# Pinning TensorE's order around seven block products, and taking up the first bank's sum behind the third copy

## The chip, the cores and the metric

The kernel runs on one core of a Trainium2 chip. The time is the device time of the whole program in microseconds (us); lower is better. TensorE (PE) multiplies matrices into PSUM banks, VectorE (DVE) and ScalarE (ACT) do elementwise work, and SyncE (SP) issues the transfers. Each engine takes its instructions in a fixed order and waits at an instruction until its operands are ready.

## The reference

Two batches of 768 tokens pass a decayed block attention ("retention", 8 heads of 64), and its output goes through two feed-forward layers, one with Mish and one with ELU:

```python
x = attn_out.transpose(0, 2, 1, 3).reshape(1536, 512)
h = x @ moe_w_in                     # 512 -> 2048
g = h * np.tanh(softplus(h))         # Mish
x = g @ moe_w_out                    # 2048 -> 512
h = x @ moe2_w_in
g = np.where(h > 0, h, np.exp(np.minimum(h, 0)) - 1)   # ELU
return g @ moe2_w_out
```

## The kernel before

**Products.** Tokens come in three blocks of 512 (t = 0, 1, 2). Every operand is kept as two fp32r tiles, high part and low part, and each 128x128 by 128x512 product is made of three matmuls: high by high, high by low, low by high. In the text "a product" means one such matmul of 512 columns; a bank is one 128x512 PSUM tile.

**Groups and units.** A layer's 2048 inner columns are four groups of four slices of 128. A group's work is cut into units in the list `seq`: an `in` unit multiplies one slice of w_in with one token block (12 products, bank `h`, line 487), an `out` unit adds four slices through w_out (12 products, bank `y`, line 615), followed by an add into `acc` on VectorE (line 643).

**Seven block products.** In groups 1 to 3 of the first layer, token blocks 1 and 2 are not taken by `in` units. A pair of slices z (0 or 1) of a group is done by seven block products of 6 matmuls each (`block_product`, line 574), from sums of weights (tiles `s`) and sums of tokens (tiles `t2` to `t4`). They stand in four `mix` units, `MIX = ((1, 2), (6, 5), (7,), (4, 3))`. Bank 0 takes products 1, 6, 7 and 4 one on top of the other; behind 1, 6 and 7 ScalarE copies it away (`keep`, line 583), so 6 waits for the copy of 1, 7 for the copy of 6, and 4 for the copy of 7. Bank 1 takes product 2, bank 2 takes 5 and 3. `done` (line 587) adds a bank to a copy on VectorE, applies Mish on ScalarE and splits the result in two (`split_g`, line 161 for the low part). For z = 0 the banks come from the `y` pool and are called `mby`, for z = 1 from the `h` pool, `mbh`.

In `seq` the units of such a group stand as: `in` 0, 1, 2; mix 0 to 2 of z = 0; `in` 3; mix 3; `out` 0, 1, 2 of token block 0; mix 0 to 2 of z = 1; `out` 3; mix 3; then the other `out` units.

**Weights.** A pair of weight slices is loaded raw (512 KB a slice) and split in two by `w_steps`: VectorE lines 119, 123, 125, 129, 132, 136 and 139, then ScalarE line 143 writes the high part, then VectorE line 146 the low part. `w0` is a pair of w_in slices, `w1` a pair of w_out slices. The tables `PAIRS` and `at` say after which unit a pair is begun.

**Order.** A scheduler lays out each engine's instructions ahead of time: an instruction that it takes to be not ready yet lets later ones go first. An instruction marked with `keep_in_program_order` keeps its place against the other marked ones of its engine. Before the change only the attention's instructions are marked.

Of the kernel before, what the change touches and what calls it, by code (L numbers as in the profile page):

```python
# [18 lines left out]
def kernel(  # L19
# [12 lines left out]
    nc = tc.nc  # L32
# [430 lines left out]
    def open_late():  # L463
# [11 lines left out]
            )  # L475
        acc.extend(late["y"].tile([P, KD, TB], F32, name=f"acc{t}") for t in range(NTB))

    def mm_in(s, i):
        l, g, t = steps[s]
        w = wts[l, 0, g * G + i]  # L480
        h = (late["psH"] if entered[0] % 4 else psH).tile([P, TB], F32, tag="h", name="h")
        entered[0] += 1
        for kk in range(KD):
            wa, wb = (w[:, n, kk * P:(kk + 1) * P] for n in range(2))
            xa, xb = xh[t][:, kk], xl[t][:, kk]
            for n, (lt, rt) in enumerate(((wa, xa), (wa, xb), (wb, xa))):
                nc.tensor.matmul(  # L487
                    h, lhsT=lt, rhs=rt,
                    start=(kk == 0 and n == 0), stop=(kk == KD - 1 and n == 2),
                )  # L490
        return h
# [11 lines left out]
    def split_g(s, i):  # L503
        g, gg = mid.pop((s, i)), g_tile(s, i)
        in_two((gg[:, 0], gg[:, 1]), g)
        gt[s, i] = gg

    def mish(s, i, h):
        mid[s, i] = tp.tile([P, TB], F32, tag="e", name="g32", bufs=ES)
        nc.scalar.activation(out=mid[s, i], in_=h, func=AF.Mish)  # L510
# [10 lines left out]
    mx = {}  # L521
# [30 lines left out]
    def block_product(g, z, x):  # L552


        w = [wts[0, 0, g * G + 2 * z + j] for j in range(2)]
        sm = sums[g, z]
        def of(j, h):
            return [w[j][:, n, h * 2 * P:(h + 1) * 2 * P] for n in range(2)]
        a = {1: of(0, 0), 2: of(0, 1), 4: of(1, 1)}.get(x)
        if a is None:  # L560
            y = {5: 0, 6: 1, 7: 2, 3: 3}[x]
            a = [sm[:, n, y] for n in range(2)]
        b = mx["b"][x]
        bank = {1: 0, 6: 0, 7: 0, 4: 0, 2: 1, 5: 2, 3: 2}[x]
        fresh = x in (1, 2, 5)
        if fresh:
            pool, tag = ((late["psY"], "y"), (late["psH"], "h"))[z]
            mx[z, bank] = pool.tile([P, TB], F32, tag=tag, name="mb" + tag)
        ps = mx[z, bank]
        for kk in range(2):  # L570
            ha, la = (t[:, kk * P:(kk + 1) * P] for t in a)
            hb, lb = (t[:, kk] for t in b)
            for n, (lt, rt) in enumerate(((ha, hb), (ha, lb), (la, hb))):
                nc.tensor.matmul(  # L574
                    ps, lhsT=lt, rhs=rt, start=fresh and kk == 0 and n == 0,
                    stop=kk == 1 and n == 2, skip_group_check=True,
                )
        s1, s2 = g * NTB + 1, g * NTB + 2
        i1, i2 = 2 * z, 2 * z + 1

        def keep(y):
            mx[z, "c", y] = tp.tile([P, TB], F32, tag="e", name="c", bufs=ES)
            nc.scalar.activation(out=mx[z, "c", y], in_=ps, func=AF.Copy)  # L583

        def done(y, s, i):
            c = mx[z, "c", y]
            nc.vector.tensor_tensor(out=c, in0=c, in1=ps, op=ALU.add)
            nc.scalar.activation(out=c, in_=c, func=AF.Mish)
            mid[s, i] = c
            split_g(s, i)  # L590

        if x in (1, 6, 7):
            keep({1: 1, 6: 2, 7: 3}[x])
        if x == 2:
            done(1, s1, i1)
        elif x == 3:
            done(2, s2, i1)
        elif x == 4:
            mish(s1, i2, ps)
            split_g(s1, i2)  # L600
        if x == 7:
            ps = mx[z, 2]
            done(3, s2, i2)

    def mm_out(s, d, cols):
        l, g, t = steps[s]
        y = late["psY"].tile([P, TB], F32, tag="y", name="y")[:, cols]
        for i in range(G):
            w = wts[l, 1, g * G + i]
            gg = gt[s, i]  # L610
            a, b = (w, gg) if l == 0 else (gg, w)
            a = [a[:, n, d * P:(d + 1) * P] for n in range(2)]
            b = [b[:, n, cols] for n in range(2)]
            for n, (lt, rt) in enumerate(((a[0], b[0]), (a[0], b[1]), (a[1], b[0]))):
                nc.tensor.matmul(  # L615
                    y, lhsT=lt, rhs=rt,
                    start=(i == 0 and n == 0), stop=(i == G - 1 and n == 2),
                )
        return y

    def all_out(s):

        l, g, t = steps[s]
        ys = [late["psY"].tile([P, TB], F32, tag="y", name="y") for _ in range(KD)]
        for i in range(G):
            w, gg = wts[l, 1, g * G + i], gt[s, i]
            for d, y in enumerate(ys):
                a = [w[:, n, d * P:(d + 1) * P] for n in range(2)]
                for n, (lt, rt) in enumerate(((a[0], gg[:, 0]), (a[0], gg[:, 1]), (a[1], gg[:, 0]))):
                    nc.tensor.matmul(  # L630
                        y, lhsT=lt, rhs=rt,
                        start=(i == 0 and n == 0), stop=(i == G - 1 and n == 2),
                    )
        for d, y in enumerate(ys):
            flush(s, d, slice(0, TB), y)

    def flush(s, d, cols, y):
        l, g, t = steps[s]
        dst = acc[t][:, d, cols]
        if g == 0:  # L640
            nc.scalar.activation(out=dst, in_=y, func=AF.Copy)  # L641
        else:
            nc.vector.tensor_tensor(out=dst, in0=dst, in1=y, op=ALU.add)  # L643
        if g < NG - 1:
            return
        if l == 0:
            nc.scalar.activation(out=xh[t][:, d], in_=dst, func=AF.Copy)
            nc.vector.tensor_tensor(
                out=xl[t][:, d], in0=dst, in1=xh[t][:, d].bitcast(F32), op=ALU.subtract
            )  # L650
        else:
            c2, b = divmod(d, B)
            r0 = b * S + (2 * t + c2) * P
            nc.sync.dma_start(out=out[r0:r0 + P, cols], in_=dst)
# [3 lines left out]
    seq = [("in", t, i) for i in range(G) for t in range(NTB)]  # L658
# [8 lines left out]
    for g in range(1, NG):  # L667
        s = g * NTB
# [15 lines left out]

    def unit(u):
        kind, s, x = seq[u]
        if kind == "mix":
            for y in MIX[x]:
                block_product(*s, y)
        elif kind == "in":  # L690
            (mish, elu)[steps[s][0]](s, x, mm_in(s, x))
            if late:
                split_g(s, x)
        else:

            if s == 0:
                if x == 0:
                    all_out(s)
                return
            ends = (0, 3 * TB // 4, TB) if u == len(seq) - 1 else (0, TB)  # L700
            for c0, c1 in zip(ends, ends[1:]):
                cols = slice(c0, c1)
                flush(s, x, cols, mm_out(s, x, cols))
# [11 lines left out]
    for g in range(2 * NG):  # L715
        for y in range(4):
            u = PAIRS[g][y] if g in PAIRS else 92 + (g - 4) * 24 + (-18, -6, -9, -3)[y]
# [38 lines left out]
    def first_units():  # L756
        with tc.issue_after(made[-2].ins):
            for _ in todo:
                pass
        for u in range(EARLY):  # L760
            unit(u)
            weights_at(u)
# [5 lines left out]
    for u in range(EARLY, len(seq)):  # L768
        unit(u)
        weights_at(u)  # L770
# [32 lines left out]
```

## Time and profile before

| | |
|---|---|
| median of 3 runs | 576.34 us (576.29 to 577.77) |
| profiled execution | 576.26 us |
| its span, first to last instruction | 573.7 us |
| TensorE busy | 567.1 us, 99% |
| VectorE busy | 455.3 us, 79% |
| ScalarE busy | 246.0 us, 43% |
| granted TensorE clock | 1.000 |

Shares are of the span. 2.56 us of the execution lie outside the span. A busy share is a mean over stages; the attention takes the first 54 us, the first layer runs to some 340 us, the second to the end.

### The profile page before, as it was taken

The page shows a single profiled execution, that of the slowest core. Times are in us where ns is not written, and L with a number is a line of the kernel's source. Part 1 is how long each engine was busy: PE and PEld are TensorE (multiplying, and loading weights), DVE is VectorE, ACT ScalarE, POOL GpSimd, SP SyncE. Part 2 cuts the span into 40 slices and gives each one's busy share as a digit, 9 for nine tenths or more (in the row PEclk, how much of TensorE's full clock was granted, in tenths as well). Part 3 has the DMA queues.
Part 4 walks back from the last instruction along what each step waited for, and adds up shares of the span by engine and source line. Part 5 has one row for each costly group of instructions (what it writes and reads, how often), then busy time and mean ns, then how long its engine had stood idle before and what let it go on. Part 6 is the DMA issues. An engine that isn't in the chain of part 4 may idle for free.

```text
span 573.7 us, 7842 instructions
## 1 busy us (share of the span) xinstructions
PE 567.1 (99%) x3198; PEld 474.7 (83%) x3198; DVE 455.3 (79%) x628; ACT 246.0 (43%) x389; POOL 18.8 (3%) x28
## 2 busy tenths in 40 slices
PE   8999999999999999999999999999999999999997
PEld 7998888887888888888888888888888888888886
DVE  7779999999999979889989899898999634244232
ACT  3655553453542352422646447445325425225220
POOL 5330000000000000000000000000000000000000
PEclk9999999999999999999999999999999999999999
DMA  9998242111312421032222204404312000000112
GB/s 188 200 209 217 81 140 74 73 75 61 93 67 75 146 75 37 37 121 83 90 75 72 75 0 148 146 1 147 100 48 74 0 1 0 1 0 1 73 56 91
DMA packets 61042, 46.63 MB, mean 81 GB/s; under 512 B 38864, under 2 KB 55504, under 8 KB 61008
## 3 DMA queue, kind: packets, MB, share of 16 engines
q1 hardware_dynamic: 60864, 46.14, 26.7%
q8 instruction: 25, 0.41, 0.3%
q14 instruction: 9, 0.07, 0.0%
q10 hardware_dynamic: 144, 0.00, 0.0%
HBM read 43.00 MB, written 3.15 MB: 80 GB/s over the span
## 4 chain that ended last, share of the span: by engine, by line
PE 97%; SPq 1%; DMA 1%; issue 0%; ACT 0%; DVE 0%
PE y L615 44%; PE h L487 34%; PE mby L574 5%; PE mbh L574 5%; PE o L341 4%; PE y L630 2%; PE sc L327 2%; SPq L205 1%; DMA qn<-in_q_dram 1%; PE Tp L283 1%; PE st L373 1%; ACT c L583 0%; DVE acc L643 0%
## 5 line engine op out<-in xcount | busy, mean ns | idle before, releaser
L487 PE MATMUL h<-xh,w 128*128 128x512 f32 x576 | 181.7, 389 | 0.0
L615 PE MATMUL y<-w,g 128*128 128x512 f32 (+2 forms) x588 | 133.5, 386 | 0.0
L615 PEld LDWEIGHTS y<-w,g 128*128 128x128 f32 x588 | 109.5, 188 | 22.0
L487 PEld LDWEIGHTS h<-xh,w 128*128 128x128 f32 x576 | 108.1, 188 | 22.6 <-issue 0.2
L615 PE MATMUL y<-g,w 128*128 128x512 f32 x528 | 124.9, 389 | 0.0
L615 PEld LDWEIGHTS y<-g,w 128*128 128x128 f32 x528 | 99.1, 188 | 20.6
L487 PE MATMUL h<-xl,w 128*128 128x512 f32 x288 | 112.0, 389 | 0.0
L643 DVE TENSOR_TENSOR acc<-acc,y 128x512 f32<-128x512 f32 (+1 forms) x73 | 48.8, 677 | 41.5 <-PE y L615 41.4
L514 ACT ACTIVATE e<-h 128x512 f32<-128x512 f32 x48 | 28.6, 598 | 87.5 <-PE h L487 85.8
L487 PEld LDWEIGHTS h<-xl,w 128*128 128x128 f32 x288 | 54.1, 188 | 11.2
L516 DVE SCALAR_TENSOR_TENSOR e<-e,h 128x512 f32<-128x512 f32 x48 | 32.7, 685 | 25.9 <-ACT e L515 25.9
L146 DVE TENSOR_TENSOR w<-m,w 128x1024 fp32r<-128x1024 f32 (+2 forms) x35 | 39.5, 1130 | 8.5 <-ACT w L143 8.5
L143 ACT ACTIVATE w<-m 128x1024 fp32r<-128x1024 f32 (+2 forms) x35 | 34.4, 983 | 24.6 <-PE y L615 16.6
L161 DVE TENSOR_TENSOR g<-e,g 128x512 fp32r<-128x512 f32 x48 | 33.0, 689 | 12.2 <-ACT g L160 12.0
L160 ACT ACTIVATE g<-e 128x512 fp32r<-128x512 f32 x48 | 30.2, 630 | 24.3 <-DVE e L516 24.1
L129 DVE SCALAR_TENSOR_TENSOR raw<-raw,m 128x1024 int32<-128x1024 int32 (+2 forms) x35 | 39.4, 1130 | 0.2
L136 DVE SCALAR_TENSOR_TENSOR m<-raw,m 128x1024 f32<-128x1024 uint32 (+2 forms) x35 | 39.2, 1129 | 0.2
L139 DVE TENSOR_TENSOR m<-raw,m 128x1024 f32<-128x1024 f32 (+2 forms) x35 | 39.1, 1128 | 0.2
L510 ACT ACTIVATE g<-h 128x512 f32<-128x512 f32 x24 | 14.4, 598 | 44.8 <-PE h L487 44.8
L515 ACT ACTIVATE e<-e 128x512 f32<-128x512 f32 x48 | 30.0, 630 | 1.1
L641 ACT ACTIVATE acc<-y 128x512 f32<-128x512 f32 x24 | 13.9, 599 | 28.2 <-PE y L615 21.7
L119 DVE TENSOR_SCALAR m<-raw 128x1024 int32<-128x1024 int32 (+2 forms) x35 | 22.1, 644 | 3.5 <-DMA raw<-in_moe_w_out_dram 2.1
(105 smaller groups left out, 576.6 us busy)
## 6 DMA issues: line engine op xcount, KB each, us to landing
raw<-in_moe_w_out_dram SPq DMA_DIRECT2D x32, 512.0 KB, 4.1
raw<-in_moe_w_in_dram SPq DMA_DIRECT2D x31, 512.0 KB, 4.9
vn<-in_v_dram SPq DMA_DIRECT2D x12, 256.0 KB, 5.6
kn<-in_k_dram SPq DMA_DIRECT2D x11, 256.0 KB, 5.1
qn<-in_q_dram SPq DMA_DIRECT2D x11, 256.0 KB, 5.4
out_dram<-acc SPq DMA_DIRECT2D x11, 256.0 KB, 2.0
raw<-in_moe_w_in_dram SPq DMA_DIRECT2D x2, 256.0 KB, 4.9
kn<-in_k_dram SPq DMA_DIRECT2D x2, 128.0 KB, 3.3
```

Source lines behind the costliest of these rows:

```text
L129: yield nc.vector.scalar_tensor_tensor(out=b, in0=b, scalar=-0x40000000, in1=m, op0=ALU.bitwise_and, op1=ALU.bitwise_or)
L136: yield nc.vector.scalar_tensor_tensor(out=mf, in0=lw, scalar=2.0 ** -52, in1=mf, op0=ALU.mult, op1=ALU.mult)
L139: yield nc.vector.tensor_tensor(out=mf, in0=bf, in1=mf, op=ALU.add)
L143: nc.scalar.activation(out=w0, in_=mf, func=AF.Copy)
L146: yield nc.vector.tensor_tensor(out=w1, in0=mf, in1=w0.bitcast(F32), op=ALU.subtract)
L160: nc.scalar.activation(out=t[0], in_=x, func=AF.Copy)
L161: nc.vector.tensor_tensor(out=t[1], in0=x, in1=t[0].bitcast(F32), op=ALU.subtract)
L487: nc.tensor.matmul(h, lhsT=lt, rhs=rt, start=(kk == 0 and n == 0), stop=(kk == KD - 1 and n == 2),)
L516: nc.vector.scalar_tensor_tensor(out=e, in0=e, scalar=-1.0, in1=h, op0=ALU.add, op1=ALU.max)
L574: nc.tensor.matmul(ps, lhsT=lt, rhs=rt, start=fresh and kk == 0 and n == 0, stop=kk == 1 and n == 2, skip_group_check=True,)
L615: nc.tensor.matmul(y, lhsT=lt, rhs=rt, start=(i == 0 and n == 0), stop=(i == G - 1 and n == 2),)
L643: nc.vector.tensor_tensor(out=dst, in0=dst, in1=y, op=ALU.add)
```

## The change

A list `fixed` is filled while a unit is written out if that unit, the one ahead of it in `seq` or the one behind it is a `mix` unit. In that case each product of the unit is marked to keep program order. And `done(1)`, which adds bank 1 to the first copy, is called behind the third copy (after product 7) and not right after product 2.

```diff
+    fixed = []
+
+    def product(*args, **kw):
+        ins = nc.tensor.matmul(*args, **kw)
+        if fixed:
+            tc.keep_in_program_order(ins)
+
     def mm_in(s, i):
...
-                nc.tensor.matmul(
+                product(
...
         if x in (1, 6, 7):
             keep({1: 1, 6: 2, 7: 3}[x])
-        if x == 2:
-            done(1, s1, i1)
-        elif x == 3:
+        if x == 3:
             done(2, s2, i1)
         elif x == 4:
             mish(s1, i2, ps)
             split_g(s1, i2)
         if x == 7:
-            ps = mx[z, 2]
-            done(3, s2, i2)
+            for y, bank, s, i in ((3, 2, s2, i2), (1, 1, s1, i1)):
+                ps = mx[z, bank]
+                done(y, s, i)
...
     def unit(u):
         kind, s, x = seq[u]
+        fixed[:] = [1 for y in seq[max(u - 1, 0):u + 2] if y[0] == "mix"]
```

`mm_in`, `block_product` and `mm_out` call `product` in place of the matmul. The number of instructions on each engine stays the same, and so does the order up to the first mix unit of group 1. Lines shift: 487, 574 and 615 print as 481 in the order of the changed kernel, 583 as 590, 587 as 594, 643 as 649.

**Place one: TensorE, group 1, the first `out` units (`y_1701`, `y_1715`, `y_1729`).** `w1_1530` and `w1_1580` are the group's two pairs of w_out slices, `g_...` the split slices of token block 0; the third product of a slice is the first that reads the low part of its weights. Before:

```order
L574 MATMUL mby_1612<-t3_1298,s_1392 128x512 x6
L615 MATMUL y_1701<-g_1559,w1_1530 128x512 x2
L615 MATMUL y_1715<-g_1559,w1_1530 128x512 x2
L574 MATMUL mby_1612<-t4_1299,w0_1374 128x512 x6
L574 MATMUL mbh_1772<-xh2_66,s_1414 128x512
L574 MATMUL mbh_1772<-xl2_69,s_1414 128x512
L574 MATMUL mbh_1772<-xh2_66,s_1414 128x512 x2
L574 MATMUL mbh_1772<-xl2_69,s_1414 128x512
L574 MATMUL mbh_1772<-xh2_66,s_1414 128x512
L615 MATMUL y_1701<-g_1559,w1_1530 128x512
```

Now:

```order
L481 MATMUL y_1701<-g_1559,w1_1530 128x512 x2
L481 MATMUL y_1715<-g_1559,w1_1530 128x512 x2
L481 MATMUL y_1701<-g_1559,w1_1530 128x512
L481 MATMUL y_1701<-g_1577,w1_1530 128x512 x3
L481 MATMUL y_1701<-g_1609,w1_1580 128x512 x2
L481 MATMUL y_1715<-g_1559,w1_1530 128x512
L481 MATMUL y_1715<-g_1577,w1_1530 128x512 x3
L481 MATMUL y_1715<-g_1609,w1_1580 128x512 x2
```

The mix products that stood between the second and the third product of `y_1701` have moved ahead of it (z = 0) or behind it (z = 1), and the second pair of w_out slices is read 8 products after the first and not 39. Before, the first product after the group's `in` units 0 and 1 was product 1 of the mix; now the `in` unit 2 (`h_1594`, weights `w0_1396`) stands there whole. From that place to the first `y_1701` are 66 products in both kernels, and to its third product, the first that reads the low part of `w1_1530`, 70 products now.

**Place two: TensorE, group 1, the first `in` unit of group 2 (`h_1998`, weights `w0_1792`).** Before:

```order
L574 MATMUL mbh_1743<-t3_1298,s_1414 128x512 x6
L615 MATMUL y_1850<-g_1630,w1_1530 128x512 x3
L615 MATMUL y_1850<-g_1687,w1_1530 128x512 x3
L615 MATMUL y_1850<-g_1761,w1_1580 128x512 x3
L487 MATMUL h_1998<-xh0_64,w0_1792 128x512
L487 MATMUL h_1998<-xl0_67,w0_1792 128x512
```

Now:

```order
L481 MATMUL mbh_1752<-xh1_65,w0_1396 128x512 x2
L481 MATMUL mbh_1752<-xl1_68,w0_1396 128x512
L481 MATMUL mbh_1752<-xh1_65,w0_1396 128x512
L481 MATMUL h_1998<-xh0_64,w0_1792 128x512
L481 MATMUL h_1998<-xl0_67,w0_1792 128x512
L481 MATMUL mbh_1743<-t2_1297,s_1414 128x512 x6
```

It begins 39 products earlier, between products 2 and 6 of z = 1. From the third product of `y_1701` to it are 44 products (10 of `y_1701`, 10 of `y_1715`, 12 of `y_1729`, 12 of `mbh`).

**Place three: VectorE, up to the low part of `w1_1530`.** Before:

```order
L161 TENSOR_TENSOR g_1609<-g32_1607,g_1609 128x512
L132 TENSOR_SCALAR m_1581<-raw_1405 128x1024
L139 TENSOR_TENSOR m_1531<-raw_1383,m_1531 128x1024
L161 TENSOR_TENSOR g_1630<-c_1619,g_1630 128x512
L136 SCALAR_TENSOR_TENSOR m_1581<-raw_1405,m_1581 128x1024
L146 TENSOR_TENSOR w1_1530<-m_1531,w1_1530 128x1024
```

Now (`g_1609` stands further ahead, `g_1630` is called `g_1658`):

```order
L594 TENSOR_TENSOR c_1649<-c_1649,mby_1636 128x512
L132 TENSOR_SCALAR m_1581<-raw_1405 128x1024
L139 TENSOR_TENSOR m_1531<-raw_1383,m_1531 128x1024
L136 SCALAR_TENSOR_TENSOR m_1581<-raw_1405,m_1581 128x1024
L161 TENSOR_TENSOR g_1653<-c_1649,g_1653 128x512
L161 TENSOR_TENSOR g_1658<-c_1619,g_1658 128x512
L594 TENSOR_TENSOR c_1634<-c_1634,mby_1636 128x512
L161 TENSOR_TENSOR g_1676<-g32_1674,g_1676 128x512
L139 TENSOR_TENSOR m_1581<-raw_1405,m_1581 128x1024
L146 TENSOR_TENSOR w1_1530<-m_1531,w1_1530 128x1024
```

From the low part of `w0_1396` on, the instructions ahead of this line 146 are those of before and five more: the adds `c_1649` and `c_1634`, the splits `g_1653` and `g_1676`, and line 139 of `m_1581`. Behind it follow two splits (`g_1687`, `g_1698`), line 146 of `w1_1580`, and the steps of `w0_1792`: lines 119, 123, 125, 129, an add, 132, an add, 136, 139.

## Rows read from the trace of the kernel before

**Rows 1.** The page's span and busy times.

```profile
span 573.7 us, 7842 instructions
PE 567.1 (99%) x3198; PEld 474.7 (83%) x3198; DVE 455.3 (79%) x628; ACT 246.0 (43%) x389; POOL 18.8 (3%) x28
```

**Rows 2.** Chain that ended last: start us, length us, what.

```profile
137.86 1.37 PE mby L574 x6
139.90 1.65 PE mby L574 x6
142.47 1.43 PE mby L574 x6
...
179.05 10.88 PE y L615 x48
...
270.85 1.44 PE mby L574 x6
...
428.70 10.88 PE h L487 x48
```

**Rows 3.** Busy time by stretch: each engine's us and count, clock, DMA share, GB/s.

```profile
9.00:10.00 1.00, 0.52 (x7) 0.33 (x6) 1.00 (x2) 0.73 (x1) 1.00 (x2) 1.00 1.34 224
126.00:138.00 12.00, 12.00 (x55) 9.94 (x54) 11.79 (x17) 4.71 (x8) 0.00 (x0) 1.00 0.01 3
138.00:146.00 8.00, 7.31 (x32) 5.59 (x31) 7.21 (x10) 4.70 (x8) 0.00 (x0) 1.00 0.54 166
146.00:160.00 14.00, 14.00 (x63) 11.60 (x62) 13.96 (x21) 6.50 (x11) 0.00 (x0) 1.00 0.36 126
```

**Rows 4.** TensorE's timeline in group 1: start us, length us, what, idle before.

```profile
125.45 0.39 PE L574 MATMUL mby<-xh,w 128*128 128x512 f32 x1
...
137.69 1.52 PE L574 MATMUL mby<-t,s 128*128 128x512 f32 x6
139.90 1.65 PE L574 MATMUL mby<-t,s 128*128 128x512 f32 x6 [0.69 <-ACT c L583]
141.39 1.07 PE L615 MATMUL y<-g,w 128*128 128x512 f32 x4
```

**Rows 5.** ScalarE's timeline in the same place.

```profile
124.10 1.05 ACT L143 ACTIVATE w<-m 128x1024 fp32r<-128x1024 f32 x1
...
139.25 0.60 ACT L583 ACTIVATE c<-mby 128x512 f32<-128x512 f32 x1 [2.06 <-PE mby L574]
139.75 1.05 ACT L143 ACTIVATE w<-m 128x1024 fp32r<-128x1024 f32 x1
```

**Rows 6.** VectorE's timeline in group 1.

```profile
119.22 0.69 DVE L132 TENSOR_SCALAR m<-raw 128x1024 int32<-128x1024 int32 x1
119.94 1.23 DVE L136 SCALAR_TENSOR_TENSOR m<-raw,m 128x1024 f32<-128x1024 uint32 x1
121.20 1.22 DVE L139 TENSOR_TENSOR m<-raw,m 128x1024 f32<-128x1024 f32 x1
...
125.18 1.23 DVE L146 TENSOR_TENSOR w<-m,w 128x1024 fp32r<-128x1024 f32 x1
...
139.25 0.68 DVE L161 TENSOR_TENSOR g<-c,g 128x512 fp32r<-128x512 f32 x1
139.86 1.22 DVE L136 SCALAR_TENSOR_TENSOR m<-raw,m 128x1024 f32<-128x1024 uint32 x1
140.99 1.22 DVE L146 TENSOR_TENSOR w<-m,w 128x1024 fp32r<-128x1024 f32 x1
...
146.54 1.22 DVE L146 TENSOR_TENSOR w<-m,w 128x1024 fp32r<-128x1024 f32 x1
```

**Rows 7.** VectorE and TensorE at the mix of group 3.

```profile
259.14 0.68 DVE L587 TENSOR_TENSOR c<-c,mby 128x512 f32<-128x512 f32 x1
...
255.73 0.39 PE L574 MATMUL mby<-xh,w 128*128 128x512 f32 x1
```

**Rows 8.** TensorE's timeline at the start of the attention.

```profile
1.05 3.36 PE L267 MATMUL warm<-idle 128*128 128x128 f32 x14 [1.05 <-DVE idle L218]
4.34 0.47 PE L283 MATMUL Tp<-ident,kn 64*128 64x64 f32 x4
...
8.59 0.71 PE L267 MATMUL warm<-idle 128*128 128x128 f32 x4
```

More of the change, by code (lines that the diff above doesn't have):

```diff
@@ L573, in block_product @@
             for n, (lt, rt) in enumerate(((ha, hb), (ha, lb), (la, hb))):
-                nc.tensor.matmul(
+                product(
                     ps, lhsT=lt, rhs=rt, start=fresh and kk == 0 and n == 0,
@@ L614, in mm_out @@
             for n, (lt, rt) in enumerate(((a[0], b[0]), (a[0], b[1]), (a[1], b[0]))):
-                nc.tensor.matmul(
+                product(
                     y, lhsT=lt, rhs=rt,
```

## The prediction

> **What bounds the kernel now.** I read the page's busy times first: TensorE is busy for 99% of the span, VectorE for 79% [rows 1]. A busy matmul row can hide time, so next the chain that ended last, for the pace: 48 products take 10.88 us at 179 us and at 429 us alike, whichever bank they fill, which is 0.2267 us a product [rows 2]. The reader should see that TensorE works at one pace from the first layer to the end, so order alone saves nothing: only places where it leaves that pace count. Six products take 1.36 us; at 137.69 us six of them are followed only after 2.21 us, and the six behind the wait take 1.49 us until the next row [rows 4]. So a wait costs its length and 0.13 us more behind it. The losses are 0.85 + 0.13 us there, 0.07 us at 142.47 and 0.08 us at 270.85 [rows 2, 4]: **1.13 us is all that the pinning could win back**. The wait is product 7's for the copy of product 6 [rows 4, 5].
>
> Then the stretches: in the mix of group 1 VectorE is busy for 11.79 of 12 us, 7.21 of 8 and 13.96 of 14 [rows 3]. TensorE is on time there only because the scheduler can put products without a late operand in front. That is what the change forbids.
>
> **What the change does, part by part.** All sums are against the profiled execution of 576.26 us, which is within 0.02% of the median 576.34. No instruction is added or removed, on the transfer queues neither, so TensorE's work stays the same and I add waits.
>
> *The wait for the third copy* goes. Product 7's copy is now covered by the 12 products of `in` 3, 2.72 us. Products 6 and 7 stand six products behind the one that is copied: their operand bank is needed 0.23 + 1.36 = 1.59 us after that product's last matmul starts. The copy came free 139.90 - 138.83 = 1.07 us after it at the old wait (138.83 is 137.69 + 5 x 0.2267) [rows 4, 5]. The cover leaves 0.52 us if ScalarE is free, so I price this at 0. Gain: 1.13 us.
>
> *The low part of `w1_1530`* (place one) is the main cost. The anchor is the product at 125.45 us, which both kernels reach alike [rows 4]. 70 products later, at 125.45 + 70 x 0.2267 = 141.32 us, TensorE wants the first low part of the group's w_out weights. VectorE wrote that tile from 140.99 us before [rows 6]. Five instructions now stand ahead of it besides those of before (place three): four of 512 columns, 0.61 us each from start to start (139.25 to 139.86), and one line 139, 1.13 us as line 136 of its kind (139.86 to 140.99) [rows 6]. VectorE had next to no idle time in that stretch [rows 3], so nothing absorbs them: 4 x 0.61 + 1.13 = 3.57 us, start 144.56, end 145.78 with its 1.22 us, product at 145.83 (0.05 us from a writer's end to the product, as 139.85 to 139.90 [rows 4, 5]). Loss: 145.83 - 141.32 + 0.13 = **4.64 us**. Smaller waits ahead are inside it: `h_1594` now begins at 125.45 and its third product needs the low part that ends at 126.41 [rows 6], 0.6 us; the high part of `w1_1530`, read by the first `y_1701`, some 2 us. Bounds: if only the four short ones cost, 3.5; if each of the five pays the 1.26 us that dependent steps take (119.94 to 121.20 [rows 6]), 7.4. I take the rows' pace, since each of the five stands behind unrelated work.
>
> Before, the same tile was no limit because mix products stood between, and the second pair (146.54 us, [rows 6]) had 31 products, 7 us, more time than now.
>
> *The weights of group 2* (place two). VectorE goes on from 144.56 us: line 146 1.13, two splits 1.22, line 146 of `w1_1580` 1.13, to 148.04. Then the steps of `w0_1792` one behind the other: three short ones at 0.72 us (119.22 to 119.94 [rows 6]), 2.16; line 129 1.13; add, 132, add 1.83; 136 1.26; 139 1.22 to its end, 155.64. ScalarE's high part takes 1.05 [rows 5], and with 0.05 on either side `h_1998` starts at 156.79. TensorE arrives 44 products behind 145.83, at 155.80 + 0.13 = 155.93. Loss 0.86 + 0.13 = **0.99 us**. Bounds: 0 if the adds come late enough to be passed, 2.0 if the raw load is late too.
>
> *Group 3* reads a split token slice late: the second product of the fourth slice in `out` 0, 74 products behind the first of the mix, 255.73 + 16.77 = 272.50 us by the rows of before [rows 7]. From VectorE's first add of that mix at 259.14 us [rows 7] the new order has 12 instructions at 0.61 and 5 at 1.13 ahead of that split (12.97 us, steps of two weight pairs most of them): start 272.11, end 272.80, product at 272.85. Loss 0.35 + 0.13 = **0.48 us** (0 to 1.3, one line 139 more or less). In group 2 VectorE has one weight pair in hand there: four steps at 0.61 and two at 1.13 fewer, two of some 0.4 more, so the split is some 3.9 us earlier and costs 0.
>
> *The later `done(1)`* moves little: the scheduler may still let the add go where its operands are ready, and VectorE's order shows it there (`c_1619` ahead of `c_1649`). It takes its split behind that of `c_1649`. Bank 1 is held no longer for that; 0.
>
> Sum: 4.64 + 0.99 + 0.48 - 1.13 = +4.98 us, **581.2 us**. Nothing gives it back, since TensorE has no idle time behind it to shorten.
>
> **A clock that falls.** After the new wait TensorE makes four products (0.9 us) between two waits of some 2 us. The rows show the granted clock at 1.00, the 2.4 GHz level, even where TensorE was busy for 0.52 of a microsecond [rows 3]; and at the very start, out of idleness, 14 small matmuls take 3.36 us where later four take 0.71: about twice the pace [rows 8]. So the lower level costs up to half of the 4 us before the fast pace, 2 us. By the Trainium skill (TensorE: Matmul & The Clock Gate, HAM oscillation — how this bites in real kernels) waits for operands between bursts of matmuls send the clock back to half rate, so that the next burst starts slow. By that rule the time would be 583.2; the 0.85 us wait of before left the clock at 1.00 [rows 3], so the trace has no such case.
>
> **The rivals.**
> 1. *Not slower.* VectorE gets the w_out tile done in time, so that the removed waits are all that is left: 576.26 - 1.13 = 575.1. It decides at 140.0 us: line 146 has to start there for the product at 141.32. For it speaks that ScalarE has room (43%) and that the tile's own steps end early; against it, that it started at 140.99 even without the five instructions, and that VectorE takes them in a fixed order. 5%.
> 2. *Half of it.* Waits of the five on one another fall into gaps, or the clock of the loads shifts, and the tile is 2 us earlier: 579.2. 6%.
> 3. *The clock falls* for one such stretch behind the waits: 581.2 + 2.0 = 583.2. 10%.
> 4. *The close copies fail.* 12 copies (two in each of six mixes) have 0.52 us of room; an older 1.05 us instruction on ScalarE ahead of one takes up to 0.53 from TensorE. If half of them meet it in full, 6 x 0.53 = 3.2 us more: 584.4. Against it: ScalarE is idle ahead of the copy at 139.25 for 2.06 us [rows 5]. 6%.
> 5. *The change does nothing to the waits*, that is the pinned order is what stood there: excluded by place one.
>
> **How the numbers follow.** The forecast as worked out has 70%, and its own range is 580.2 to 582.5 (the terms together 1.0 less or 1.3 more). The other 3% lie outside all cases. The range that leaves out no more than 2 in 10 reaches down to rival 2 and up to rival 3: 579.2 to 583.4. A measurement can tell about 0.3%, 1.73 us: slower means over 578.0, faster under 574.6. Rival 1 lies within; so slower 92%, same 6%, faster 2%.
>
> **What would show each step.** The wait of product 7 at 139.90 is gone. In group 1 TensorE waits for ScalarE's line 143 and then VectorE's line 146 at the first `y`, with the last wait ending near 145.8; then once at the first `h` of group 2, near 156.8; and shortly near 277 (272.5, later by 4.64 + 0.99 less the 1.05 won by then). From 360 us on the rows equal those of before, later by 5.0 us. VectorE's line 146 starts near 144.5. Wrong it would be if that line starts near 141, if the granted clock shows less than 1.00 around 146 us, or if copies of line 590 show up among TensorE's waits.

## The result, and the profile after

The changed kernel takes 582.03 us (median of 4 runs, 581.23 to 583.25), the kernel before 576.33 in the same comparison. The ratio is 1.0101, with a 95% interval of 1.0086 to 1.0115: slower by 1%. Of the changed kernel the profiled execution is the quickest of the four, 581.23 us with a span of 578.7.

The page's span and busy times after, which answer to [rows 1]:

```profile
span 578.7 us, 7844 instructions
PE 570.0 (98%) x3198; PEld 476.7 (82%) x3198; DVE 454.0 (78%) x628; ACT 246.5 (43%) x389; POOL 18.8 (3%) x28
```

The span is 5.0 us longer with the same 3198 matmuls. The two instructions more are waits for a semaphore (three more on ScalarE, one fewer at TensorE's weight loads); the work on each engine is the same. TensorE's share has only gone from 99% to 98%, and its busy time has even grown by 2.9 us for the same work; 1.7 us of that growth lie in the first 54 us, the attention, which the change does not touch. These rows do not say where the time went; the starts of the products do.

TensorE's waits after (engine, tile and line, releaser: us in total, times, longest):

```profile
PE y L481 <- DVE w L146: 1.7, 1, 1.7
PE y L481 <- ACT w L143: 1.6, 1, 1.6
...
PE h L481 <- ACT w L143: 0.7, 1, 0.7
PE h L481 <- DVE w L146: 0.4, 1, 0.4
```

Each of the four stands once, and all four releasers write split weights: line 143 the high part, line 146 the low one. No copy (line 590) is among them. TensorE's timeline gives their places; it answers to [rows 4]:

```profile
126.55 0.73 PE L481 MATMUL h<-xh,w 128*128 128x512 f32 x2 [0.39 <-DVE w L146]
...
142.97 1.20 PE L481 MATMUL y<-g,w 128*128 128x512 f32 x4 [1.62 <-ACT w L143]
...
145.89 7.56 PE L481 MATMUL y<-g,w 128*128 128x512 f32 x32 [1.71 <-DVE w L146]
...
156.84 0.50 PE L481 MATMUL h<-xh,w 128*128 128x512 f32 x1 [0.67 <-ACT w L143]
```

The bracket is shorter than the loss, since the row ahead counts as busy for 0.39 us where the next product could start after 0.2267. Measured from start to start against 0.2267 us a product, the four cost 0.55, 1.78, 1.88 and 0.83 us, and the product behind each wait another 0.11. The wait at 139.90 of before [rows 4] is gone.

VectorE's timeline around the second and third of them, to hold against [rows 6]:

```profile
141.07 1.29 DVE L161 TENSOR_TENSOR g<-c,g 128x512 fp32r<-128x512 f32 x2
142.27 0.69 DVE L594 TENSOR_TENSOR c<-c,mby 128x512 f32<-128x512 f32 x1
142.87 0.69 DVE L161 TENSOR_TENSOR g<-g,g 128x512 fp32r<-128x512 f32 x1
143.47 1.23 DVE L139 TENSOR_TENSOR m<-raw,m 128x1024 f32<-128x1024 f32 x1
144.61 1.23 DVE L146 TENSOR_TENSOR w<-m,w 128x1024 fp32r<-128x1024 f32 x1
```

VectorE has no gap from 141.07 to the end of line 146 at 145.84, and TensorE's product starts 0.05 us behind that. Before, this line 146 started at 140.99 [rows 6]. Now two splits, an add, another split and a line 139 stand right ahead of it.

The chain that ended last now leaves TensorE in group 1 for VectorE's queue and comes back at the first `h` of group 2; far behind, its long rows stand as in [rows 2]:

```profile
143.56 1.14 DVE m L139
144.70 1.14 DVE w L146
...
154.47 1.24 DVE m L139
155.70 0.02 issue
155.72 1.07 ACT w L143
156.79 0.04 issue
156.84 0.74 PE h L481 x2
...
433.66 10.88 PE h L481 x48
```

The last row was at 428.70 before [rows 2]: 4.96 us later, which is the loss of this execution (581.23 - 576.26 = 4.97). Nothing is lost or won behind that point. The stretches of [rows 3] after:

```profile
126.00:138.00 12.00, 11.61 (x51) 9.50 (x51) 11.79 (x17) 5.59 (x9) 0.00 (x0) 1.00 0.02 10
138.00:146.00 8.00, 4.67 (x20) 3.23 (x19) 8.00 (x11) 6.95 (x11) 0.00 (x0) 1.00 0.43 134
146.00:160.00 14.00, 13.33 (x58) 10.58 (x59) 13.83 (x20) 2.53 (x4) 0.00 (x0) 1.00 0.43 149
```

From 138 to 146 us TensorE makes 20 products where it made 32, while VectorE is busy all 8 us: in this stretch VectorE has become the bound. The granted clock is 1.00 throughout, here. It was not so in every execution; experiment 2 comes to that.

### The profile page after: what moved, and what is told of

It reads as the page before. It is cut to its first block, busy times and chain, and to the rows that moved or that the text cites. A ratio compares the mean times of both kernels' runs of the same rounds, so it can differ in the third digit from the quotient of the medians.

```text
span 578.7 us, 7844 instructions
## 1 busy us (share of the span) xinstructions
PE 570.0 (98%) x3198; PEld 476.7 (82%) x3198; DVE 454.0 (78%) x628; ACT 246.5 (43%) x389; POOL 18.8 (3%) x28
## 4 chain that ended last, share of the span: by engine, by line
PE 91%; DVE 7%; ACT 1%; issue 1%; DVEq 0%
PE y L481 41%; PE h L481 33%; PE mbh L481 4%; PE o L341 4%; PE sc L327 2%; PE y L636 2%; PE mby L481 2%; PE Tp L283 1%; DVE raw L129 1%; DVE m L136 1%; DVE g L161 1%; PE st L373 1%; PE warm L267 1%; DVE w L146 1%; DVE m L139 1%
## 5 line engine op out<-in xcount | busy, mean ns | idle before, releaser
L481 PE MATMUL y<-g,w 128*128 128x512 f32 x528 | 122.7, 390 | 3.4 <-DVE w L146 1.7
```

The source lines that it names most:

```text
L481: ins = nc.tensor.matmul(*args, **kw)
```

## Experiments

Diffs are against the changed kernel. "The marks" are those that make TensorE keep its program order.

**1. Which half of the change costs.** `done_only` has no marks and takes up the first bank's sum late; `pin_only` has all marks and takes it up in the old place. The edit of `done_only`:

```diff
 def unit(u):
     kind, s, x = seq[u]
-    fixed[:] = [1 for y in seq[max(u - 1, 0):u + 2] if y[0] == "mix"]
```

> No pins, done(1) called behind product 7. Theory: the scheduler lays the work out almost as before, with the 0.85 us wait for the third copy: 576.1 to 576.4 us, granted clock 1.000. Rival (the later done(1) is what costs): some 581 us.

> All pins, but done(1) is called right after product 2 as before. Theory: the same waits in group 1, since the same instructions of VectorE stand ahead of the low part of the w_out weights; 580.5 to 581.3 us. Rival (the later done(1) is what disturbs VectorE's order): back to 576 to 577 us.

Measured: `done_only` 576.0 us (10 runs), ratio 1.0001 (0.9991 to 1.0010); `pin_only` 582.11 (4 runs), ratio 1.0104 (1.0089 to 1.0119). TensorE's timeline of `done_only` has the old wait at the old place:

```profile
139.84 1.65 PE L481 MATMUL mby<-t,s 128*128 128x512 f32 x6 [0.69 <-ACT c L590]
```

The marks are the whole loss; the later sum does nothing by itself. `pin_only` lies above the 580.5 to 581.3 expected; the clock, of which experiment 2 tells, fell in all four of its executions.

**2. Which group costs.** `pin_g1` marks only around the mix of group 1, `pin_g23` only around those of groups 2 and 3 (`y[1][0] > 1`). The edit of `pin_g1`:

```diff
-    fixed[:] = [1 for y in seq[max(u - 1, 0):u + 2] if y[0] == "mix"]
+    fixed[:] = [
+        1 for y in seq[max(u - 1, 0):u + 2] if y[0] == "mix" and y[1][0] == 1
+    ]
```

> The products are pinned around the mix units of group 1 alone; the later done(1) stays. Theory (the pinned order asks for group 1's w_out weights before VectorE has written them): TensorE's waits at the third product of in 2, at the first out unit and at group 2's first in unit stay (0.6, 1.8, 1.9 and 0.9 us with what follows each), only group 3's 0.4 us goes; profiled time 580.8 us. Rival (every pinned stretch costs about the same, by close copies and lost freedom): a third of the loss, some 578 us. If the clock rival explains why the changed kernel's other runs are up to 2 us longer than its profiled one, some runs here show a granted clock under 1.000 too.

> The products are pinned around the mix units of groups 2 and 3 alone; group 1 stands as before the change. Theory: group 1's own waits of before stay (1.05 us), group 3 adds its 0.4 us at the split slice: 576.7 us, granted clock 1.000 in all runs. Rival (every pinned stretch costs the same): two thirds of the loss, some 579.6 us.

Measured: `pin_g1` 581.86 us (580.61 to 582.53), ratio 1.0092 (1.0076 to 1.0109); `pin_g23` 576.76, ratio 1.0008 (0.9998 to 1.0017). The loss sits in group 1. The profile of `pin_g1` also shows what that of the changed kernel does not; TensorE's timeline of `pin_g1`:

```profile
142.93 1.20 PE L481 MATMUL y<-g,w 128*128 128x512 f32 x4 [1.62 <-ACT w L143]
145.84 10.37 PE L481 MATMUL y<-g,w 128*128 128x512 f32 x32 [1.72 <-DVE w L146]
156.05 0.39 PE L481 MATMUL mbh<-xh,w 128*128 128x512 f32 x1
```

The waits are the same two, but the 32 products behind them take 10.37 us, not the 7.56 of the profile after. The stretches of `pin_g1` (columns as in [rows 3]) say why:

```profile
143.00:146.00 3.00, 1.28 (x5) 0.75 (x5) 3.00 (x4) 2.60 (x4) 0.00 (x0) 0.84 0.62 206
146.00:148.00 2.00, 2.00 (x5) 1.62 (x6) 2.00 (x3) 0.00 (x0) 0.00 (x0) 0.50 0.85 265
148.00:152.00 4.00, 4.00 (x11) 3.08 (x11) 3.35 (x5) 0.00 (x0) 0.00 (x0) 0.51 0.35 122
152.00:156.00 4.00, 4.00 (x19) 3.32 (x18) 3.35 (x5) 0.00 (x0) 0.00 (x0) 1.00 0.00 0
```

During the second wait the granted clock falls to 0.50, the 1.2 GHz level; it stays there from 145.07 to 151.90 us, and 14 products run at a pitch of 0.427 us, 0.20 more each. They cost 2.8 us (14 x 0.20); but the first `h` of group 2 comes later by that much, and its wait of 0.94 us disappears: 1.9 us net.

**3. The changed kernel once more**, for its clock (`after_again`, no edit).

> The changed kernel once more, for its granted clock. If the fall of the clock behind the two close waits is what separates its median from the forecast, the executions divide: those with a mean granted clock of 0.999 at about 581.2, those with 0.994 to 0.997 at 581.6 to 583.3, and a trace of the latter shows the products behind the second wait at a pitch of 0.427 us and no wait at the first product of group 2. If the clock plays no part, all lie within 0.3 us of each other.

Measured: 581.47 us, ratio 1.0092 (1.0077 to 1.0107). With the four runs of the result, the eight executions by mean granted clock:

| mean granted clock | executions, us |
|---|---|
| 0.999 or 1.000 | 581.15, 581.23 |
| 0.997 | 581.03, 581.61, 581.79 |
| 0.994 | 582.22, 582.45, 583.25 |

Its profile is that of the 582.22 us execution. Two of its stretches:

```profile
143.00:146.00 3.00, 1.30 (x5) 0.73 (x4) 3.00 (x5) 2.19 (x3) 0.00 (x0) 0.65 0.58 170
146.00:148.00 2.00, 2.00 (x6) 1.61 (x5) 2.00 (x3) 0.00 (x0) 0.00 (x0) 0.50 1.01 339
```

As expected where the clock is lowest: 0.50 behind the second wait, 0.427 us a product there, and no wait at the first `h` of group 2. In the traces a mean of 0.994 goes with 6.8 us at the lower level, and 0.997 (`one_wait` below) with 3.4; the 0.999 of the profiled execution of the result comes from its last 1.5 us, in which TensorE no longer works. Executions at 0.994 take 1.0 to 2.1 us more than those at 1.000. At 0.997 the loss is within the scatter (from 0.2 less to 0.6 more), so that the division that I expected blurs there. The kernel before shows 0.999 or 1.000 in all the runs that stood beside these experiments.

**4. Is it the queue on VectorE?** `no_add_g1` leaves out the three adds of a bank to a copy in group 1's first pair of slices, so that part of the result isn't computed. In the changed kernel all three are done ahead of the low part of `w1_1530`, and two of them are among the five instructions that the change put there.

```diff
-            nc.vector.tensor_tensor(out=c, in0=c, in1=ps, op=ALU.add)
+            if (g, z) != (1, 0):
+                nc.vector.tensor_tensor(out=c, in0=c, in1=ps, op=ALU.add)
```

> The changed kernel without the three adds of a bank onto a copy in group 1, z = 0: that part of the result is left out. TensorE's products stay. VectorE has three instructions of 0.61 us fewer in its queue, and in the built order only one of the five that the change put ahead of the first w_out pair's low part is left there (line 139 of the second pair now follows it). Theory (VectorE's queue sets the wait): that low part starts near 141.1 and not 144.6 us, the wait of 1.9 us falls to 0.6 or less, the second pair's weights then bring waits of some 2 us; 578 to 579.5 us with the clock at 1.00. Rival (ScalarE's copies or PSUM banks set it): 581.

Measured: 578.51 us, one run. Its timeline of TensorE:

```profile
145.06 1.20 PE L481 MATMUL y<-g,w 128*128 128x512 f32 x4 [0.71 <-ACT w L143]
146.91 3.47 PE L481 MATMUL y<-g,w 128*128 128x512 f32 x14 [0.65 <-DVE w L146]
```

And of VectorE:

```profile
140.97 1.21 DVE L146 TENSOR_TENSOR w<-m,w 128x1024 fp32r<-128x1024 f32 x1
142.10 0.68 DVE L161 TENSOR_TENSOR g<-g,g 128x512 fp32r<-128x512 f32 x1
142.70 1.22 DVE L139 TENSOR_TENSOR m<-raw,m 128x1024 f32<-128x1024 f32 x1
```

The low part of `w1_1530` starts at 140.97 us again, as before the change [rows 6], since the three adds are gone and a line 139 and a split now stand behind it. The first `out` unit waits for it only 0.26 us. The two waits above are those for the second pair, whose line 139 that is: 0.88 and 0.82 us from start to start. The wait at group 2's first `h` is gone.

**5. Or is it when TensorE asks?** `out_later` keeps all marks and all of VectorE's work, but lists the units of group 1 so that the out units stand behind more mix products.

```diff
+        if g == 1:
...
+            seq.append(("mix", (g, 0), 3))
+            seq.append(("mix", (g, 1), 0))
+            seq.append(("mix", (g, 1), 1))
+            seq.append(("mix", (g, 1), 2))
+            seq.append(("out", s, 0))
+            seq.append(("mix", (g, 1), 3))
...
```

> All pins and the later done(1), but in group 1 the list of units puts in 2 behind mix 2 of z = 0 and the out units behind mix 2 of z = 1, so that TensorE first reads the w_out weights 96 products behind the first of the mix and not 66: 30 products, 6.8 us. Theory (the pins cost only because the weights are asked for early): the waits of 1.8 and 1.9 us go, at most 2 us of waits for the second pair of weights stay, no h unit of group 2 stands in the mix; 575.6 to 577.6 us and granted clock 1.000. Rival (the pinned order itself costs): 581 us.

Measured: 576.94 us, ratio 1.0011 (1.0002 to 1.0020), clock 0.999 to 1.000 in all 10 runs. What is left in group 1, by TensorE's timeline, are the waits for the second pair of w_out slices, 1.01 and 0.70 us from start to start:

```profile
149.17 0.73 PE L481 MATMUL y<-g,w 128*128 128x512 f32 x2 [0.85 <-ACT w L143]
150.43 1.20 PE L481 MATMUL y<-g,w 128*128 128x512 f32 x4 [0.53 <-DVE w L146]
```

So it is both sides of one meeting: shorten the queue or ask later, and the wait shrinks.

**6. One long wait in place of two.** In `one_wait` all marks stand, and the out units are listed so that high and low part of the second pair are asked for two products apart.

```diff
+        if g == 1:
...
+            seq.append(("mix", (g, 1), 1))
+            seq.append(("out", s, 0))
+            seq.append(("mix", (g, 1), 2))
+            seq.append(("out", s, 1))
+            seq.append(("mix", (g, 1), 3))
...
```

> Every order pinned and the first bank's sum taken up late, but group 1's seven blocks stand as in0, in1, mixes 0 to 2 of unit 0, in2, its last mix, in3, then unit 1's mixes 0 and 1, out 0, mix 2, out 1, mix 3, out 2, out 3. The high and the low part of the second w_out pair are asked for with two products between them, so the 1.78 and 1.88 us waits of the changed kernel become one long wait of about 2.5 us and one of about 0.9; the copy of the second partial, with nothing in front of it now, may add 1 us; group 3 keeps 0.4. Main theory (the order decides which weights are asked for early): 576.3 + 2.5 + 0.9 + 1.0 + 0.4 = about 581, with a mean granted clock of 0.999 if the clock only falls behind two waits with four products between. Rival (any idle stretch this long in that place lets the clock fall): 582 to 583 with a mean granted clock of 0.994 to 0.997. If the waits are not in group 1's order at all: 576.

Measured: 580.27 us, ratio 1.0067 (1.0050 to 1.0084); clock 0.996 or 0.997 in three of four runs, 1.000 in the fourth. Its timeline of TensorE:

```profile
150.00 0.73 PE L481 MATMUL y<-g,w 128*128 128x512 f32 x2 [2.21 <-ACT w L143]
151.37 2.08 PE L481 MATMUL y<-g,w 128*128 128x512 f32 x4 [0.64 <-DVE w L146]
```

The waits came as expected (2.37 and 0.81 us from start to start), while the 1.0 us allowed for a copy did not come. The clock falls here too: it stands at 0.50 from 150.95 us, during the second wait, to 154.36, and products run at 0.427 us from 151.96 us on. So four products between the waits are no condition for it, and the rival was right on the clock; on the time it was wrong, as the fall lasts 3.4 us here against 6.8 in `pin_g1`. Whether one wait alone would do it, this run doesn't tell: two products and a second wait stood behind the long one. The timeline of `pin_only` (experiment 1) does:

```profile
143.19 1.70 PE L481 MATMUL y<-g,w 128*128 128x512 f32 x4 [1.83 <-ACT w L143]
```

These are the four products between its two waits, and they take 1.70 us where they take 1.20 in `pin_g1`: the clock falls at 143.65, when only the first wait of the pair (1.99 us from start to start) and two products at full pace lie behind. A second wait is not needed.

**7. Marks on the mix units alone** (`pin_mix`): the in and out units around them are left to the scheduler.

```diff
-    fixed[:] = [1 for y in seq[max(u - 1, 0):u + 2] if y[0] == "mix"]
+    fixed[:] = [1] if kind == "mix" else []
```

> Pins on the mix units alone, not on the in and out units beside them. Theory: in 2 can go behind the mix again and the out units are free, so the waits for the w_out weights shrink to under 1 us; the waits for close copies come back at 0.9 us where the mix has nothing between; 577 to 579.5 us. Rival (the pins in the mix are what costs): 581.

Measured: 580.13 us, one run: missed. What I had counted is there: waits for copies, 0.85 us in group 1 and 0.40 in group 3, and for the w_out weights, 0.22 us for a high part. Not counted were 0.61 us in group 3, where product 3 waits for VectorE's add (line 594) of the sum in its bank, and this, in the timeline:

```profile
307.49 3.02 PE L481 MATMUL y<-g,w 128*128 128x512 f32 x12 [1.33 <-DVE acc L649]
```

An out unit of group 3 waits for its own bank, which is free only when VectorE has added what it held to `acc`: 1.50 us from start to start. Another 0.8 us was lost ahead of the first layer, whose first product starts at 55.51 us and not at 54.69 as in the profile after; in the attention of this execution TensorE waits 1.1 us for its v tiles and 0.8 for its q tiles, and the profile after has neither wait. The clock stays at 1.00 behind all of these waits.

**8. No marks, but the units of group 1 listed in turn** (`weave_g1`): the mixes and the in and out units alternate.

```diff
+        if g == 1:
...
+            seq.append(("mix", (g, 0), 0))
+            seq.append(("in", s, 2))
+            seq.append(("mix", (g, 0), 1))
+            seq.append(("mix", (g, 0), 2))
+            seq.append(("in", s, 3))
+            seq.append(("mix", (g, 0), 3))
+            seq.append(("mix", (g, 1), 0))
+            seq.append(("out", s, 0))
+            seq.append(("mix", (g, 1), 1))
+            seq.append(("out", s, 1))
+            seq.append(("mix", (g, 1), 2))
+            seq.append(("out", s, 2))
+            seq.append(("mix", (g, 1), 3))
+            seq.append(("out", s, 3))
...
-        fixed[:] = [1 for y in seq[max(u - 1, 0):u + 2] if y[0] == "mix"]
```

> No pins; done(1) stays behind product 7; in group 1 alone the list of units is woven another way (in 0, in 1, mix 0, in 2, mix 1, mix 2, in 3, mix 3 of z = 0; then each mix unit of z = 1 followed by one out unit). Between products 1, 6 and 7 of z = 0 stand 16, 20 and more products in place of 10 and none, so the wait for the third copy (0.85 us and 0.13 behind it) has cover, and the w_out weights are first read where they were before the change. Theory: 576.3 - 1.0 to 1.1 = 575.2 us, granted clock 1.000. Rival (pace, not waits, decides): 576.3.

Measured: 574.85 us (11 runs, 574.36 to 575.94) beside 576.22 of the kernel before, ratio 0.9976 (0.9967 to 0.9985): faster than both kernels. TensorE's timeline from product 6 to product 4; the rows between the first two are products of `h` and `mbh`:

```profile
133.22 1.52 PE L481 MATMUL mby<-t,s 128*128 128x512 f32 x6
...
139.11 1.52 PE L481 MATMUL mby<-t,s 128*128 128x512 f32 x6
140.47 1.07 PE L481 MATMUL y<-g,w 128*128 128x512 f32 x4
141.38 1.59 PE L481 MATMUL mby<-t,w 128*128 128x512 f32 x6
```

Twenty products now stand between products 6 and 7 (from 134.58 to 139.11 us), where before there was none [rows 4], and product 7 no longer waits for the copy of 6. The list of TensorE's waits in this trace has none in the layers. Of the 1.13 us that the pinning could win back, the 0.85 of this wait and the 0.13 behind it are won here without it.

**9. The marks on top of that list** (`pin_weave`): does the list of units or the marking make the loss?

```diff
 def unit(u):
     kind, s, x = seq[u]
+    fixed[:] = [1 for y in seq[max(u - 1, 0):u + 2] if y[0] == "mix"]
```

(against `weave_g1`)

> The list of units of the woven kernel (574.85 us without marks), with the marks of the changed kernel on top. TensorE now takes those units in exactly the order of the list: the first out unit of group 1 stands 78 products behind the first mix product, its third product 80, the second pair of w_out slices 84. By the changed kernel's rows the low part of the first pair is there some 1.1 us earlier than its 145.78, since one line 139 of 1.13 us now stands behind it, so its wait is 144.7 - 143.6 = 1.1 us; the second pair's line 139 comes later by that and by two short steps, so its high part ends near 148.1 against a need at 145.6, 2.5 us, and its low part waits 0.9 more. Group 3 pays 0.3 again, the copies nothing. Main theory (what the marks take away is the putting of products without a late operand in front): 574.9 + 0.3 + 1.2 + 2.6 + 1.0 = 580, from 578.5 to 581.5. Rival (the marks do no harm where the list of units fits; the loss came from the old list): 574.9.

Measured: 582.42 us, ratio 1.0112 (1.0095 to 1.0129), clock 0.994 in all four runs. The waits of its timeline:

```profile
144.78 1.20 PE L481 MATMUL y<-g,w 128*128 128x512 f32 x4 [1.21 <-DVE w L146]
148.20 3.34 PE L481 MATMUL y<-g,w 128*128 128x512 f32 x6 [2.23 <-ACT w L143]
151.34 2.77 PE L481 MATMUL mbh<-t,s 128*128 128x512 f32 x6
```

From start to start they are 1.37 and 2.40 us, where I had 1.1 and 2.5. Above the 580 expected, and above its range of 578.5 to 581.5, lies the clock: it stands at 0.50 from 147.38 us, during the second wait, to 154.21, and the six products of the last row take 2.56 us from start to start where six in full pace take 1.36. The same list of units is the fastest without the marks and among the slowest with them, 7.6 us apart: what costs is that another product may no longer be put in front of one whose weights are late. That the marks are harmless where the list asks late enough is shown by `out_later`.

## Why the prediction was right

The forecast was 581.2 us; the profiled execution took 581.23, the median of its four runs is 582.03 and that of the four later ones 581.47. The range held all three. That the profiled execution meets the forecast to 0.03 us is luck in two ways: it is one of the two among eight in which the clock did not fall, and terms that came out 0.26 us too large stand against 0.24 us that were in no term.

- **Only departures from the pace count:** right. Nearly all of the loss is in a handful of starts: five waits with the 0.11 us behind each are 5.85 us, less the 1.13 won 4.72 of the 4.96. Of the rest 0.09 lie ahead of the first layer, and the others are hundredths behind the waits. From 360 us on the rows are 4.96 us later, 5.0 forecast.
- **The third copy's wait, 1.13 us won:** right. No wait for line 590 is left after, and the kernels without marks in group 1 (`done_only`, `pin_g23`) have it still.
- **The low part of `w1_1530`, 4.64 us:** right in place and size. The product was put at 145.83 and started at 145.89, VectorE's line 146 at 144.56 against 144.61. The three waits up to there cost 0.55, 1.78 and 1.88 us, with 0.11 behind each 4.54. That VectorE's queue and TensorE's early demand make it together is shown from both sides (experiments 4 and 5).
- **The weights of group 2, 0.99 us:** 0.83 + 0.11 = 0.94, at 156.84 (forecast 156.79). That VectorE's queue makes it is read from the chain; no run tests it by itself. And this term isn't independent, as I treated it: where the clock falls, it vanishes.
- **Group 3, 0.48 us:** 0.26 + 0.11 = 0.37, at 276.06 us and so a microsecond before the place that I named, since the first mix product stands at 259.02, 3.3 and not 4.6 us behind its old 255.73 [rows 7].
- **The later `done(1)`, 0:** right by `done_only`; with the marks, `pin_only` at 582.11 is no different either.
- **A clock that falls, 10%:** this is the step that was mis-sized, in its chance. I took it as something that the kernel does or does not do; in fact it differs from execution to execution, and it came in six of eight of the changed kernel and in all eight of `pin_g1` and `pin_only`. A clock under 1.00 around 146 us, which I had named as a sign of being wrong, is there in the trace of `after_again` (0.65 from 143 to 146 us, 0.50 from 146 to 148). From one wait of 0.85 us that left the clock alone I argued to 10%, although the new waits were twice as long and close together. The Trainium skill (TensorE: Matmul & The Clock Gate, HAM oscillation — how this bites in real kernels) tells of a kernel whose matmuls come in bursts between waits for transfers, and whose every burst starts slow; its waits are longer than any here. Taken to hold for these waits too, that rule would have given 583.2; the traces of `pin_g1`, `after_again` and `pin_weave` agree with it (0.50 behind the waits), the profiled execution of the changed kernel does not (1.00 with the same waits).
- **The price of that fall, 2.0 us:** about right (1.0 to 2.1 more at a mean clock of 0.994), but not by its working: the slow products cost 2.8 us, and 0.94 of that is hidden where the wait of group 2 vanishes. The rows that I took the lower pace from do not give "about twice" as I put it (14 in 3.36 us are 0.24 each, four in 0.71 are 0.18, and the trace of before has no record of the clock ahead of 5.04 us); from start to start it is 0.213 us in the first and 0.112 at the end of the second, which does.
- **The other rivals:** VectorE was not in time (1), the tile was not 2 us earlier (2), and no copy failed its cover (4).

Not settled: why the same waits leave the clock at 1.00 in some executions and not in others. Where it falls, the moment differs too: 0.5 us behind the end of the first of the two waits in `pin_only`, 1.4 in `after_again`, 2.1 in `pin_g1`. Nothing here tells these apart ahead of time.

## What to carry to other kernels

Where one engine is busy for 99% of the span, its order may be good only because late operands are passed over, and fixing the order then brings their waits out. Before pinning an order, count the distance of each first use from its writer in the new order, on the writer's queue too. And the loss of one wait was won here by listing the units in turn, without forbidding the scheduler to move them.

## What the runs showed of the hardware that was not expected

- The granted clock fell to 0.50, though TensorE worked at full pace up to the first of two close waits. It fell during the second wait in `pin_g1` and `after_again` (1.8 and 1.9 us with four products between), `one_wait` (2.4 and 0.8 with two) and `pin_weave` (1.4 and 2.4 with four), and in `pin_only` already behind the first, of 2.0 us. It stayed there for 6.8 us (3.4 in `one_wait`), products at 0.427 us against 0.2267. Two waits of 1.0 and 0.7 us (`out_later`) and one of 1.5 (`pin_mix`) left it at 1.00, and so did, in the profiled execution of the result, the very waits of 1.8 and 1.9.
- A fall of the clock can pay for itself in part: the slower products hid a wait of 0.94 us that stood behind them.
- The product behind one that waited comes 0.11 us late, in every trace here where the clock was at 1.00; at 0.50 it was 0.16 to 0.17 (0.591 to 0.594 us from start to start against 0.427).
